# Banded attention with block summaries, then two feed-forward nets: the mask moves into the score products, the block means of v to TensorE

## The chip, the cores and the metric

One core of a Trainium2 chip runs the whole program. The metric is device time in microseconds for one execution. TensorE is called PE below (its sequencer PEq), VectorE DVE, ScalarE ACT, GpSimd POOL, SyncE SP; SP issues nearly all DMAs.

## The reference, cut to what matters

```python
q, k, v: (2, 8, 768, 64); block, window = (32, 16)
k_sum = k.reshape(B, H, nb, block, D).max(axis=3)        # 24 blocks of 32 positions
v_sum = v.reshape(B, H, nb, block, D).mean(axis=3)
scores_l = scale * q @ k^T, kept where |i - j| < 16, else -1e9
scores_s = scale * q @ k_sum^T + log(block)
a = softmax over [scores_l, scores_s]
attn = a @ [v, v_sum]
x = attn as (1536, 512)
h = x @ w_in;  x = (h - tanh(h)) @ w_out                  # d_ff 2048
h = x @ w2_in; out = (h * tanh(softplus(h))) @ w2_out
```

## The kernel before, in words

**Attention.** The 1536 positions are 12 units `u` of 128, six to a batch (`UPB`). A unit needs `kt`, its keys with 16 more at either side and two copies of the 24 block maxima `ksum`; `qt`, its queries; and `vu`, two windows of 96 values, each beside the 24 block means, so 120 rows. `qk(u)` makes the scores of 8 heads in two PSUM tiles, `s` and `tr`, one for each half `e` of the heads: 16 products, 120 columns for each of 4 heads and 2 query halves. `softmax(u, e)` lets DVE add the mask and take the maximum, one head an instruction (line 324), which moves the scores from PSUM into `aa`; ACT then takes the exponentials in `aa` (line 329). `norm` divides by the sums (DVE, then POOL at line 341), `a_trans` transposes on PE and copies to `asb`, `av` multiplies by `vu`, and `x_hi`, `x_lo` split the result into the two parts that the nets read.

**Block means of v.** `load_vt` brings a transposed copy of v in three tiles a batch, `v_sum` adds up 32 columns on DVE or POOL, `v_trans` turns the sums round on PE, ACT writes them into the `vu` buffer of the batch's first unit, and `v_fill` copies them by DMA into the other two of the three `vu` buffers, where they stay for the batch.

**Order.** Nothing reorders: each engine runs its instructions as the code issues them. A loop over steps `j` issues `qk(j/2)` at even `j`, half `e` of a unit's softmax at `j = 2u+1+e`, `norm(u)` at `2u+3`, `a_trans(u, e)` at `2u+5+e`, `av(u)` at `2u+7`, `x_hi(u)` at `2u+8`. `at(j, ...)` hangs loads and sums behind a step, `before_av` puts work ahead of `av`. The first product of the nets (`more_in`) stands at `j = 24`, behind `qk(11)`, `a_trans(9, 0)` and `av(8)`. Each of `s`, `tr`, `aT` and `x` has two PSUM buffers.

**Nets.** From there PE runs 96 steps; a step needs 12 products of 512 columns into the hidden layer and 12 out of it. The weights come as 8-byte numbers and are split on ACT, DVE and POOL, a piece of 256 columns per `conv_tick`; some ticks lie in the attention loop from `j = 19` on.

Of the kernel before, what the change touches and what calls it, by code (L numbers as in the profile page):

```python
# [2 lines left out]

# [18 lines left out]
KW = T + 2 * WIN  # L22
# [4 lines left out]
def kernel(  # L27
# [143 lines left out]
    ASB_DVE = (0, 2, 7, 11, 12, 13, 14, 15, 17, 20, 21)  # L171
    NORM_DVE = (0, 13, 21, 23)
    FILL_DVE = (0, 1, 4, 5, 6, 7, 8, 9, 11)
# [5 lines left out]
    def attention(actx):  # L179
# [7 lines left out]
        qt = [kq.tile([128, HP, 128], F32, name=f"qt{n}") for n in range(3)]  # L187
        vu = [con.tile([KA, 2, H, D], F32, name=f"vu{n}") for n in range(3)]
        masks = [con.tile([128, KA], F32, name=f"mask{m}") for m in range(3)]
# [4 lines left out]
        def constants():  # L194
            nonlocal tops
            make_identity(nc, ident)
            k_edges(0)
            for m in range(3):
                nc.gpsimd.memset(masks[m], 0.0)
                for s in range(2):  # L200
                    rows = masks[m][T * s:T * s + T]
                    nc.gpsimd.memset(rows[:, SUM[s][0]:SUM[s][1]], math.sqrt(D) * math.log(BLK))
                    reg = rows[:, WND[s][0]:WND[s][1]]

                    conds = [([[1, KW]], -1, -1), ([[-1, KW]], 2 * WIN - 1, 1)]
                    if (m, s) == (0, 0):
                        conds.append(([[1, KW]], -WIN, 0))
                    if (m, s) == (2, 1):
                        conds.append(([[-1, KW]], KW - WIN - 1, 0))
                    for pattern, base, mul in conds:  # L210
                        nc.gpsimd.affine_select(
                            out=reg, in_=reg, pattern=pattern, base=base, channel_multiplier=mul,
                            compare_op=ALU.is_ge, fill=-BIG,
                        )
            k_edges(UPB)
            tops = top_tiles(2)

        vtc, ksum, vsum = {}, {}, {}
# [4 lines left out]
        def load_k_own(u):  # L223
            nc.sync.dma_start(
# [14 lines left out]
        def load_q(u):  # L239
            nc.sync.dma_start(out=qt[u % 3], in_=qt_d[u])  # L240

        def load_v(u):
            for s in range(2):
                nc.sync.dma_start(out=vu[u % 3][WND[s][0]:WND[s][1], s], in_=vw_d[u, s])

        def load_vt(b, g):
            vtc[b, g] = two.tile([128, HP, 256], F32, tag="vtc", name="vtc", bufs=3)
# [510 lines left out]
```

## Time and profile before

| what | us |
|---|---|
| median of 3 runs (lowest to highest) | 603.2 (602.33 to 606.38) |
| the profiled execution | 603.07 |
| its span | 601.3 |
| PE busy in the span | 578.8 |

The profiled execution lies 0.13 us under the median and 1.8 us above its own span. Its page gives busy times, the chain that ended last and groups of like instructions; its timeline gives each instruction's start and what it waited for.

### The profile page before, as it was taken

How to read it: one execution, taken by the hardware profiler on the slowest of the kernel's cores; microseconds unless marked ns; L12 is line 12 of the kernel's file. 1: busy time of each engine (PE TensorE's matmuls, PEld its weight loads, DVE VectorE, ACT ScalarE, POOL GpSimd, SP SyncE). 2: the span in 40 equal slices, each digit the busy share in tenths (PEclk: the TensorE clock that was granted, in tenths of full speed). 3: DMA queues.
4: the chain of work that ended last, by engine and by line, in shares of the span. 5: the costliest groups of instructions: out<-in, count | busy, mean ns of one | idle time of the engine just before them, and what ended most of it. 6: DMA issues, size and time to landing. Idle time of an engine off the chain costs nothing.

```text
span 601.3 us, 9203 instructions
## 1 busy us (share of the span) xinstructions
PE 578.8 (96%) x3212; PEld 479.0 (80%) x3212; DVE 417.8 (69%) x968; ACT 328.5 (55%) x791; POOL 53.4 (9%) x109
## 2 busy tenths in 40 slices
PE   6768899999999999999999999999999999999997
PEld 5556788888888888888888888888888888888885
DVE  5797978886251222377776489997688777597785
ACT  4788878885251122367765456664464444454442
POOL 6465660000000000000000000000000000000000
PEclk9798899999999999999999999999999999999999
DMA  9997567765020000226661102100100000100001
GB/s 271 257 306 213 154 184 238 222 218 168 0 88 0 1 0 1 62 88 192 197 186 43 40 8 63 52 2 1 55 16 1 1 1 0 71 1 1 1 1 70
DMA packets 32110, 52.20 MB, mean 87 GB/s; under 512 B 3200, under 2 KB 25728, under 8 KB 32064
## 3 DMA queue, kind: packets, MB, share of 16 engines
q1 hardware_dynamic: 32064, 51.62, 28.5%
q8 instruction: 25, 0.41, 0.3%
q14 instruction: 21, 0.17, 0.1%
HBM read 48.07 MB, written 3.15 MB: 85 GB/s over the span
## 4 chain that ended last, share of the span: by engine, by line
PE 88%; DMA 4%; DVE 3%; ACT 2%; SPq 1%; issue 1%; POOL 0%; ACTq 0%
PE aT L478 7%; PE aT L479 7%; PE tr L479 7%; PE x L479 7%; PE aT L480 7%; PE tr L480 7%; PE x L480 7%; PE x L478 7%; PE tr L478 7%; PE s L479 7%; PE s L478 7%; PE s L480 7%; DMA kt<-in_kw_dram 3%; ACT aa L329 1%; DMA vtc<-in_vt_dram 1%; PE x L363 1%
## 5 line engine op out<-in xcount | busy, mean ns | idle before, releaser
L503 DVE TENSOR_TENSOR glo<-t,ghi 128x512 fp32r<-128x512 f32 x48 | 33.4, 695 | 85.4 <-ACT ghi L498 85.4
L498 ACT ACTIVATE ghi<-t 128x512 fp32r<-128x512 f32 x48 | 30.2, 629 | 96.5 <-PE tr L480 96.5
L478 PE MATMUL aT<-xhi,w 128*128 128x512 f32 x192 | 74.9, 390 | 0.0
L478 PE MATMUL s<-xhi,w 128*128 128x512 f32 x192 | 74.9, 390 | 0.0
L480 PE MATMUL s<-xhi,w 128*128 128x512 f32 x192 | 74.7, 389 | 0.0
L480 PE MATMUL aT<-xhi,w 128*128 128x512 f32 x192 | 74.7, 389 | 0.0
L479 PE MATMUL s<-xlo,w 128*128 128x512 f32 x192 | 74.7, 389 | 0.0
L479 PE MATMUL aT<-xlo,w 128*128 128x512 f32 x192 | 74.7, 389 | 0.0
L114 ACT ACTIVATE top<-raw 128x256 f16<-128x256 bf16 x128 | 61.5, 486 | 12.2 <-ACT w L132 4.8
L121 DVE SCALAR_TENSOR_TENSOR cv<-raw,top 128x256 int32<-128x256 int32 x128 | 55.4, 434 | 11.8 <-ACT top L114 7.6
L132 ACT ACTIVATE w<-cv 128x256 fp32r<-128x256 f32 x120 | 47.6, 402 | 10.7 <-DVE cv L121 9.8
L137 DVE TENSOR_TENSOR w<-cv,w 128x256 fp32r<-128x256 f32 x114 | 48.4, 426 | 0.1
L534 DVE SCALAR_TENSOR_TENSOR t<-n,r 128x512 f32<-128x512 f32 x48 | 33.1, 689 | 17.4 <-ACT r L531 17.3
L503 DVE TENSOR_TENSOR glo<-n,ghi 128x512 fp32r<-128x512 f32 x48 | 33.1, 690 | 15.5 <-ACT ghi L498 15.5
L498 ACT ACTIVATE ghi<-n 128x512 fp32r<-128x512 f32 x48 | 30.3, 632 | 24.4 <-PE tr L479 16.1
L329 ACT ACTIVATE aa<-aa,neg 128x120 f32<-128x120 f32 x96 | 36.6, 384 | 12.4 <-DVE neg L324 12.4
L480 PEld LDWEIGHTS aT<-xhi,w 128*128 128x128 f32 x192 | 36.1, 188 | 7.5
L480 PEld LDWEIGHTS s<-xhi,w 128*128 128x128 f32 x192 | 36.1, 188 | 7.5
L478 PEld LDWEIGHTS aT<-xhi,w 128*128 128x128 f32 x192 | 36.0, 188 | 7.5
L478 PEld LDWEIGHTS s<-xhi,w 128*128 128x128 f32 x192 | 36.0, 188 | 7.5
L479 PEld LDWEIGHTS s<-xlo,w 128*128 128x128 f32 x192 | 36.0, 188 | 7.4
L479 PEld LDWEIGHTS aT<-xlo,w 128*128 128x128 f32 x192 | 36.0, 188 | 7.4
(97 smaller groups left out, 1293.1 us busy)
## 6 DMA issues: line engine op xcount, KB each, us to landing
raw<-in_w_dram SPq DMA_DIRECT2D x128, 255.8 KB, 3.6
vu<-in_vw_dram SPq DMA_DIRECT2D x24, 192.0 KB, 4.9
qt<-in_qt_dram SPq DMA_DIRECT2D x12, 256.0 KB, 4.9
vtc<-in_vt_dram SPq DMA_DIRECT2D x6, 512.0 KB, 6.7
out_dram<-o SPq DMA_DIRECT2D x9, 256.0 KB, 2.0
kt<-in_kw_dram SPq DMA_DIRECT2D x6, 320.0 KB, 8.5
kt<-in_kw_dram SPq DMA_DIRECT2D x6, 256.0 KB
out_dram<-t SPq DMA_DIRECT2D x3, 256.0 KB
```

Source lines behind the costliest of these rows:

```text
L114: nc.scalar.activation(out=tops[n % len(tops)].bitcast(F16).rearrange("p (n t) -> p n t", t=2)[:, :, 1], in_=raws[n].bitcast(BF16).rearran ...
L121: nc.vector.scalar_tensor_tensor(out=tmps[n], in0=raws.pop(n).bitcast(I32).rearrange("p (n t) -> p n t", t=2)[:, :, 0], scalar=13, in1=top ...
L132: nc.scalar.activation(out=hi, in_=t, func=ACTF.Copy)
L137: (nc.gpsimd if on_pool else nc.vector).tensor_tensor(out=W[i][:, 1, o:o + PW], in0=tmps.pop(n).bitcast(F32), in1=W[i][:, 0, o:o + PW].bit ...
L329: nc.scalar.activation(out=aa[u][:, e, hp, :], in_=aa[u][:, e, hp, :], func=ACTF.Exp, scale=-1.0, bias=neg[u][:, e, hp:hp + 1], accum_out= ...
L363: nc.tensor.matmul(out=xps[u][64 * e:64 * e + 64, hp, T * s:T * s + T], lhsT=vu[u % 3][:, s, 2 * hp + e, :], rhs=asb[u, e][:, hp, T * s:T ...
L478: nc.tensor.matmul(out=out, lhsT=w[0], rhs=x[0], start=first, stop=False)
L479: nc.tensor.matmul(out=out, lhsT=w[0], rhs=x[1], start=False, stop=False)
L480: nc.tensor.matmul(out=out, lhsT=w[1], rhs=x[0], start=False, stop=last)
L498: nc.scalar.activation(out=ghi, in_=t, func=ACTF.Copy)
L503: nc.vector.tensor_tensor(out=glo, in0=t, in1=ghi.bitcast(F32), op=ALU.subtract)
L534: nc.vector.scalar_tensor_tensor(out=ts[z], in0=ns[z], scalar=2.0, in1=rs[z], op0=ALU.add, op1=ALU.mult)
```

## The change

- `qk(u)` begins with four bfloat16 products of 480 columns, `sel` times a mask, two into each score tile; the score products accumulate on top. `sel` is an identity of 64 rows over 64 rows of ones, and the mask tile carries the constant of the block scores as three bfloat16 rows whose sum is exact. There are four mask tiles, built on POOL at the start.
- `softmax` becomes `max_(u)`, two reductions over a whole score tile and a small multiplication, both halves at the first odd step, and `exps(u, e)`, which reads the scores in PSUM.
- `vt`, `v_sum` and `v_trans` go. `v_part(b)` multiplies all twelve windows of a batch by small selecting matrices (`means`) into the four 32-row parts of one PSUM tile, ACT copies it out, `v_fold(b)` adds the parts, ACT writes the means into `vu`, and `v_fill` copies them to the other five units of the batch.
- There are 8 `vu` buffers for 3 and 5 `qt` buffers for 3; `k_fill` writes both copies at once, on DVE up to unit 6, then on POOL. The loads stand in another order, half of the first keys are issued by ACT. The tables that gave some copies and normalizations to DVE or ACT go: half 1 of `asb` is DVE's, half 0 ACT's, all normalization POOL's.

```diff
@@ attention
+        NQ, NV = 5, 8
+        means = [con.tile([KA, ZC + 32], F32, name=f"means{s}") for s in range(2)]
+        masks = {z: con.tile([128, KA], BF16, name=f"mask{z[0]}{z[1]}") for z in ((0, 0), (0, 1), (1, 0), (1, 1))}
+        sel = con.tile([128, T], BF16, name="sel")
...
         def load_k_own(u):
-            nc.sync.dma_start(
+            (nc.sync, nc.scalar)[u % 2].dma_start(
...
         def k_fill(u):
-            eng = nc.vector if u in FILL_DVE else nc.gpsimd
-            for o in (0, NB + KU):
-                eng.tensor_copy(kt[u % NK][:, :, o:o + NB], ksum[u // UPB])
+            t = kt[u % NK]
+            o = bass.AP(t.tensor, t.offset, [t.ap[0], [NB + KU, 2], [KU + 2 * NB, HP], [1, NB]])
+            (nc.vector if u <= UPB else nc.gpsimd).tensor_copy(
+                o, ksum[u // UPB].unsqueeze(1).to_broadcast([128, 2, HP, NB])
+            )
+        def v_part(b):
+            p = pst("aT")
+            for k in range(UPB // 2):
+                for t in range(4):
+                    w, s = 2 * k + t // 2, t % 2
+                    nc.tensor.matmul(
+                        out=p[32 * t:32 * t + 32, :],
+                        lhsT=means[s][:, ZC - 4 * w:ZC - 4 * w + 32],
+                        rhs=vu[(b * UPB + w) % NV][:, s].rearrange("p h d -> p (h d)"),
+                        start=k == 0, stop=k == UPB // 2 - 1,
+                    )
+            vpart[b] = two.tile([128, H * D], F32, tag="vp", name="vp", bufs=1)
+            nc.scalar.activation(out=vpart[b], in_=p, func=ACTF.Copy)
+        def v_fold(b):
+            p = pst("aT")
+            nc.tensor.matmul(out=p[0:NB, :], lhsT=fold, rhs=vpart[b])
+            n = b * UPB % NV
             for s in range(2):
                 nc.scalar.activation(
-                    out=vu[0][SUM[s][0]:SUM[s][1], s].rearrange("p h d -> p (h d)"), in_=p[0:NB, :],
+                    out=vu[n][SUM[s][0]:SUM[s][1], s].rearrange("p h d -> p (h d)"), in_=p[0:NB, :],
...
@@ qk
+            for e in range(2):
+                for s in range(2):
+                    m = masks[s, int(w == (0, UPB - 1)[s])]
+                    nc.tensor.matmul(
+                        out=sc[u, e][T * s:T * s + T], lhsT=sel,
+                        rhs=m.unsqueeze(1).to_broadcast([128, HP, KA]), start=True, stop=False,
+                    )
...
+        def max_(u):
+            for e in range(2):
+                nc.vector.tensor_reduce(out=m[:, e], in_=sc[u, e], axis=AX.X, op=ALU.max)
+            nc.vector.tensor_scalar(
+                out=neg[u], in0=m, scalar1=-1.0 / math.sqrt(D), scalar2=None, op0=ALU.mult
+            )
...
-            for hp in range(HP):
-                nc.vector.tensor_tensor_reduce(
-                    out=aa[u][:, e, hp, :], in0=pv[:, hp, :], in1=m, scale=-1.0 / math.sqrt(D),
-                    scalar=3.0e38, op0=ALU.add, op1=ALU.min, accum_out=neg[u][:, e, hp:hp + 1],
-                )
             for hp in range(HP):
                 nc.scalar.activation(
-                    out=aa[u][:, e, hp, :], in_=aa[u][:, e, hp, :], func=ACTF.Exp,
-                    scale=-1.0, bias=neg[u][:, e, hp:hp + 1], accum_out=sums[u][:, e, hp:hp + 1],
+                    out=aa[u][:, e, hp, :], in_=pv[:, hp, :], func=ACTF.Exp,
+                    scale=1.0 / math.sqrt(D), bias=neg[u][:, e, hp:hp + 1],
+                    accum_out=sums[u][:, e, hp:hp + 1],
...
@@ the order of the work
+        before_av[6] = L(v_part, 0)
+        before_av[7] = L(v_fold, 0)
+        at(7, *[L(v_fill, u) for u in range(1, UPB)])
+        at(8, L(load_q, 9), L(k_sum, 6), L(k_sum, 7))
+        at(9, L(load_v, 9), L(k_sum, 8), L(k_sum, 9))
+        at(10, L(load_q, 10), L(k_sum, 10))
+        at(11, L(load_v, 10), L(k_sum, 11), L(k_fill, 6))
...
+        before_av[18] = L(v_part, 1)
+        before_av[19] = L(v_fold, 1)
+        at(19, *[L(v_fill, u) for u in range(UPB + 1, NU)])
```

PE of the kernel before between `a_trans(0, 0)` and `av(0)`: only the four transposed sums stand there, and then the fourth unit's scores (`aT` are transposes, `s` and `tr` scores, `x` the product with `vu_100`, the first `vu` buffer).

```order
L349 MATMUL aT<-ident,aa 120x128 x4
L285 MATMUL tr<-ident,vsum 24x128 x4
L310 MATMUL s<-kt_92,qt_97 64x120
...
L349 MATMUL aT<-ident,aa 120x128 x8
L363 MATMUL x<-asb,vu_100 64x64 x16
L310 MATMUL s<-kt_93,qt_98 64x120
```

PE of the changed kernel from `a_trans(0, 1)` to `qk(4)`; `vu_102` to `vu_107` are the values of the first batch's six units, `vp` the copied-out parts.

```order
L390 MATMUL aT<-ident,aa 120x128 x4
L302 MATMUL aT<-vu_102,means_110 32x512
L302 MATMUL aT<-vu_102,means_111 32x512
...
L302 MATMUL aT<-vu_107,means_111 32x512
L390 MATMUL aT<-ident,aa 120x128 x4
L313 MATMUL aT<-vp,fold 24x512
L404 MATMUL x<-asb,vu_102 64x64 x16
L339 LDWEIGHTS sel
L339 MATMUL s<-mask_113,sel 64x480
```

Twelve products of 512 columns and the fold now stand behind the fourth unit's scores and ahead of `av(0)`, `av(0)` ahead of the fifth unit's mask and scores.

DVE of the changed kernel around the maxima of the fifth unit (`max` and `neg`), from the copy `asb(1, 1)` on.

```order
L394 COPY asb<-aT 120x512
L283 TENSOR_REDUCE ksum<-kt_95 128x4x4
L283 TENSOR_REDUCE ksum<-kt_96 128x4x4
L358 TENSOR_REDUCE max<-s 128x4
L358 TENSOR_REDUCE max<-tr 128x4
L359 TENSOR_SCALAR neg<-max 128x8
```

DVE of the kernel before at the fifth unit: the maxima of its two halves stand apart, each behind one block maximum.

```order
L255 TENSOR_REDUCE ksum<-kt_90 128x4x4
L324 ISA aa,neg<-s,mask_104 128x120
L324 ISA neg 128x1
...
L375 TENSOR_TENSOR xlo_70<-x,xhi_67 128x4x128
L255 TENSOR_REDUCE ksum<-kt_91 128x4x4
L324 ISA aa,neg<-tr,mask_104 128x120
```

So a copy that waits for PE and two block maxima now stand ahead of all eight heads' maxima.

SP of the changed kernel, from the last of the loads that nothing holds up to the first fills.

```order
L253 DMA kt_95<-in_kw_dram 128x4x160
L253 DMA kt_96<-in_kw_dram 128x4x160
L253 DMA kt_89<-in_kw_dram 128x4x160
L253 DMA kt_90<-in_kw_dram 128x4x160
L253 DMA kt_91<-in_kw_dram 128x4x160
L253 DMA kt_92<-in_kw_dram 128x4x160
L276 DMA vu_108<-in_vw_dram 96x512 x2
L276 DMA vu_109<-in_vw_dram 96x512 x2
L272 DMA qt_97<-in_qt_dram 128x512
...
L324 DMA vu_103<-vu_102 24x512 x2
```

The fill that `av(1)` reads (`vu_103`) is issued behind the keys of all twelve units, eight units' values and nine units' queries (9.04 MB); before, it stood behind nine, three and six of them and three tiles of transposed v (6.88 MB).

## Rows read from the trace of the kernel before

**Rows 1.** The profile page: the span and each engine's busy time.

```profile
span 601.3 us, 9203 instructions
...
PE 578.8 (96%) x3212; PEld 479.0 (80%) x3212; DVE 417.8 (69%) x968; ACT 328.5 (55%) x791; POOL 53.4 (9%) x109
```

**Rows 2.** Stretches: busy time by engine, granted PE clock, DMA share, GB/s.

```profile
20.40:25.00 4.60, 3.48 (x41) 2.93 (x40) 1.70 (x11) 2.01 (x8) 1.75 (x2) 0.71 1.08 300
...
47.80:53.00 5.20, 4.48 (x77) 3.63 (x76) 3.90 (x22) 3.41 (x16) 1.70 (x6) 0.82 0.94 214
```

**Rows 3.** PE's timeline: start, duration, operation, count, wait before it.

```profile
41.47 0.31 PE L310 MATMUL s<-kt,qt 64*64 64x120 f32 x1
...
42.45 1.09 PE L349 MATMUL aT<-ident,aa 128*120 128x128 f32 x8
...
47.81 0.46 PE L310 MATMUL s<-kt,qt 64*64 64x120 f32 x1
...
49.62 1.09 PE L349 MATMUL aT<-ident,aa 128*120 128x128 f32 x8
...
62.11 1.15 PE L363 MATMUL x<-asb,vu 120*64 120x64 f32 x30 [1.65 <-DVE asb L353]
...
68.29 0.50 PE L478 MATMUL s<-xhi,w 128*128 128x512 f32 x1
...
71.14 0.60 PE L349 MATMUL aT<-ident,aa 128*120 128x128 f32 x4
...
76.76 0.62 PE L349 MATMUL aT<-ident,aa 128*120 128x128 f32 x4 [0.16 <-POOL aa L341]
```

**Rows 4.** ACT's timeline: the first exponential of units 0, 3, 4, 6 and 9.

```profile
11.47 0.40 ACT L329 ACTIVATE aa<-aa,neg 128x120 f32<-128x120 f32 x1 [2.44 <-DVE neg L324]
...
26.45 0.39 ACT L329 ACTIVATE aa<-aa,neg 128x120 f32<-128x120 f32 x1
...
30.43 0.39 ACT L329 ACTIVATE aa<-aa,neg 128x120 f32<-128x120 f32 x1
...
40.69 0.38 ACT L329 ACTIVATE aa<-aa,neg 128x120 f32<-128x120 f32 x1
...
57.31 0.40 ACT L329 ACTIVATE aa<-aa,neg 128x120 f32<-128x120 f32 x1 [0.59 <-DVE neg L324]
```

**Rows 5.** Groups of instructions, first 150 us: busy and mean | idle before, releaser.

```profile
L329 ACT ACTIVATE aa<-aa,neg 128x120 f32<-128x120 f32 x96 | 36.6, 384 | 12.4 <-DVE neg L324 12.4
...
L341 POOL TENSOR_TENSOR aa<-aa,rd 128x480 f32<-128x480 f32 x20 | 20.8, 1055 | 22.8 <-DVE rd L339 10.1 <-ACT aa L329 6.5 <-PE x L363 5.9
...
L375 DVE TENSOR_TENSOR xlo<-x,xhi 128x512 fp32r<-128x512 f32 x12 | 7.9, 660 | 0.0
...
L355 ACT ACTIVATE asb<-aT 120x512 f32<-120x512 f32 x13 | 7.5, 581 | 0.3 <-PE aT L349 0.3
L353 DVE COPY asb<-aT 120x512 f32<-120x512 f32 x11 | 7.4, 674 | 2.9 <-PE aT L349 2.9
...
L272 DVE TENSOR_REDUCE vsum<-vtc 128x16 f32<-128x512 f32 x7 | 4.7, 679 | 0.0
...
L211 POOL TENSOR_SCALAR_AFFINE_SELECT mask<-mask 64x96 f32<-64x96 f32 x14 | 3.7, 261 | 0.8
```

**Rows 6.** DVE's timeline: two block sums together, a small multiplication, a fill.

```profile
17.67 1.28 DVE L272 TENSOR_REDUCE vsum<-vtc 128x16 f32<-128x512 f32 x2
...
19.67 0.17 DVE L336 TENSOR_SCALAR rd<-sums 128x8 f32<-128x8 f32 x1
...
35.30 0.33 DVE L263 COPY kt<-ksum 128x96 f32<-128x96 f32 x2
```

**Rows 7.** The chain that ended last, two pieces; and the tile `vu`: shortest/median/longest ns.

```profile
0.74 0.69 SPq L224
...
14.94 8.57 DMA kt<-in_kw_dram
...
L294 SPq DMA_DIRECT2D vu<-vu x8: 714/750/892, 21.3 to 56.9; - x8
```

More of the change, by code (lines that the diff above doesn't have):

```diff
@@ L186, in attention @@
         kt = [kq.tile([128, HP, KU + 2 * NB], F32, name=f"kt{n}") for n in range(NK)]
[L187 to L189 removed]
+        NQ, NV = 5, 8
+        qt = [kq.tile([128, HP, 128], F32, name=f"qt{n}") for n in range(NQ)]
+        vu = [con.tile([KA, 2, H, D], F32, name=f"vu{n}") for n in range(NV)]
+        ZC = 4 * (UPB - 1)
+        means = [con.tile([KA, ZC + 32], F32, name=f"means{s}") for s in range(2)]
+        fold = con.tile([128, NB], F32, name="fold")
+        masks = {z: con.tile([128, KA], BF16, name=f"mask{z[0]}{z[1]}") for z in ((0, 0), (0, 1), (1, 0), (1, 1))}
+        sel = con.tile([128, T], BF16, name="sel")
         ident = con.tile([128, 128], F32, name="ident")
@@ new lines, in constants @@
+            k_edges(UPB)
+            for n in range(NV):
+                for s in range(2):
+                    (nc.vector, nc.gpsimd)[s].memset(vu[n][SUM[s][0]:SUM[s][1], s], 0.0)
+            for s in range(2):
+                nc.gpsimd.memset(means[s], 0.0)
+                cols = means[s][:, ZC + 2 * s:ZC + 2 * s + 2]
+                nc.gpsimd.memset(cols, 1.0 / BLK)
+                own = WND[s][0] + WIN
+                for pattern, base, mul in (([[-BLK, 2]], -own, 1), ([[BLK, 2]], own + BLK - 1, -1)):
+                    nc.gpsimd.affine_select(
+                        out=cols, in_=cols, pattern=pattern, base=base, channel_multiplier=mul,
+                        compare_op=ALU.is_ge, fill=0.0,
+                    )
@@ L216, in constants @@
+            nc.gpsimd.tensor_tensor(out=fold, in0=ident[:, 0:NB], in1=ident[:, 32:32 + NB], op=ALU.add)
+            for t in (2, 3):
+                nc.gpsimd.tensor_tensor(out=fold, in0=fold, in1=ident[:, 32 * t:32 * t + NB], op=ALU.add)
             tops = top_tiles(2)
-        vtc, ksum, vsum = {}, {}, {}
+        ksum, vpart = {}, {}
         def load_k(u):
@@ L388, in attention @@
         load_q(0)
-        load_vt(0, 0)
-        load_q(1)
-        load_v(0)
-        load_vt(0, 1)
-        load_q(2)
-        load_vt(0, 2)
+        for u in range(4):
+            load_v(u)
+            load_q(u + 1)
+        for u in (4, 5):
+            load_v(u)
+        for u in (6, 7):
+            load_k(u)
         constants()
```

135 lines of the change are left out of this document (52 added, 83 removed).

## Prediction

> **What bounds the kernel now.** I read the page first. PE is busy for 578.8 of 601.3 us [rows 1], and the nets' products are most of that. PE's timeline tells where the rest lies: the first product of the nets starts at 68.29 us [rows 3], and from there on PE hardly waits before the output (0.16 us ahead of the transpose at 76.76 [rows 3]). The change leaves those 96 steps as they are. So the execution lasts 603.07 - 68.29 = 534.8 us from the nets' first product on, and the question is when that product starts. Everything below is about the attention stage.
>
> In that stage no engine is full. The stretches show PE busy for 3.48 of 4.60 us and 4.48 of 5.20, with a granted clock of 0.71 and 0.82 [rows 2]; ACT needs 0.38 us for each of 96 exponentials and waits 12.4 us for DVE's maxima [rows 5]. The first exponential comes at 11.47, the fourth unit's at 26.45, the fifth's at 30.43, the seventh's at 40.69, the tenth's at 57.31 [rows 4]: 5.5 us a unit in the middle ((57.31 - 40.69) / 3). Loads fill the DMA engines early: 300 GB/s at a full share [rows 2], and one tile of keys took 8.57 us to land on the chain [rows 7].
>
> **The change part by part.** A duration runs some 0.1 us into the next instruction of its engine (two reductions of 0.68 [rows 5] take 1.28 [rows 6]), so I count 0.1 less than the means of [rows 5] for all but the exponentials.
>
> Maxima. Before, eight instructions a unit on DVE, and ACT could begin 0.3 us after the scores. Now two reductions of 480 columns; the nearest row has two of 512 in 1.28 us, and the multiplication 0.17 [rows 6]. With hand-overs 1.45 us, and ACT begins only when all are done. So the first exponential moves from 11.47 to about 12.7.
>
> Exponentials. They read PSUM, not SBUF; ACT's copies out of PSUM, 512 columns in 0.58 [rows 5], give no reason for another price, so 0.38 each, four in 1.52. What moves is when `s` and `tr` come free: after ACT, not after DVE.
>
> Mask products. PE ran twelve products of 512 columns in 71.14 - 68.29 = 2.85 us, 0.24 each [rows 3]; four of 480 cost 0.86 one behind the other and 0.43 if the two halves of the output rows run together, as those of `av` do. I take 0.65. The scores took 42.45 - 41.47 = 0.98 and, at the low level of the clock, 49.62 - 47.81 = 1.81 [rows 3].
>
> Means of v. No row has four 32-row outputs at once. 32 score instructions (16 products in two passes, four side by side) of 120 columns took 0.98 us; 24 instructions of 512 columns cost 24 x 512/120 x 0.98/32 = 3.1 us at that rate. From `av`, whose products overlap in pairs (30 instructions of 64 columns in 1.15 us [rows 3]), it is 24 x 8 x 1.15/30 = 7.4, and with no overlap some 12.4 (four times 3.1). I take 3.3, nearest to the scores, since these too lie in four parts of the output rows or of the array. The Trainium skill (TensorE: Matmul & The Clock Gate, Part 3, measured speedup) has three products of 32 output rows side by side at 2.38 times the speed of one, not 3. By that four would cost 12.4 / 3.2 = 3.9, and my forecast would be 2 us later; no run shows it yet. On ACT it adds a copy (0.50) and two copies into `vu` (0.98, as before).
>
> What goes: 3.1 MB of `vt`, 10 us of DMA at 300 GB/s [rows 2], and seven block sums on DVE, 0.64 each by [rows 6], with POOL's five. None of it stands on the chain that I follow from 12.7 on, except through the loads, which step (4) counts. The four masks, the memsets and `fold` make some 52 small instructions on POOL, 13.5 us at the 0.26 of a select [rows 5]. The first two masks wanted are done near 7 us, ahead of the first scores, and the rest ahead of the first normalization at 16 us, so they cost nothing; at one and a half times that price normalization would begin 4 us late, and the first transposes with it.
>
> Now the chain, step by step, at a granted clock of 0.91 (PE's prices times 1.1). (1) Units 0 to 2: 24 exponentials from 12.7 with a copy (0.48): ACT is free at 22.5. (2) The scores of unit 3 wait for unit 1's last exponential (18.9), the means stand behind them: scores to 20.4, transposes to 20.9, means to 24.3, copy to 24.8. ACT has waited 1.7. Unit 3 starts at 24.8, 1.6 us ahead of before (26.45 [rows 4]). (3) ACT: 1.52, a copy 0.48, both copies into `vu` 0.98: 27.8. PE: `av(0)` 1.2, masks and scores of unit 4 1.9, transposes 0.5: 31.5. DVE: the copy 0.6, two block maxima 1.28, the maxima 1.45: unit 4 starts at 34.9. Before it was 30.43: 4.5 behind. ACT has run dry at 31.2, with `x_hi(0)` and unit 3's second half done. (4) `av(1)` needs the fill, which lands behind 9.04 MB: at 300 GB/s, from an estimated 2.5 us on (the first issue stands at 0.74 [rows 7]), that is 32.6, and 1 more to land: 33.7, while PE is there at 32.1. `av(1)`, masks, scores, transposes to 37.3; DVE's copy, a block maximum, maxima: unit 5 at 40.1. The ten fills cost SP 0.75 us each to issue [rows 7]; queued behind them are only loads of values and queries for unit 8 on, 10 us early. (5) Unit 6's scores need `k_fill(6)`, which stands on DVE behind unit 5's maxima (40.0), the reciprocals 0.37, `x_lo` 0.58, a block maximum 0.62 and itself 0.33 [rows 5, 6]: 41.9. Scores 1.2, transposes 0.5, copy 0.6, maxima 1.5: unit 6 at 45.95, before 40.69 [rows 4]: 5.3 behind. (6) Then PE's round sets the pace: masks 0.7, scores 1.1, two transposes 1.2, `av` 1.2, hand-over 0.1: 4.3 us, above ACT's 3.04 + 0.48 + 0.48 = 4.0. That gives 1.2 us a unit back against 5.5: unit 9 at 58.9, and with the second batch's means (a wait of 1.2 and a copy) 60.6, before 57.31: 3.3 behind. (7) ACT: 1.52 + 0.48 + 0.98 to 63.6; `av(6)` to 64.9; two rounds of PE, each masks to `av`: the nets start at 73.6, where before had 68.29: 5.3 us late.
>
> (8) Behind that, `a_trans(11, .)` waits for POOL, which now does both halves (1.0 us each [rows 5]) among the weight pieces; before, DVE did one and PE still waited 0.16 us [rows 3]. I add 1.0.
>
> Sum: 534.8 + 73.6 + 1.0 = 609.4 us. The profiled execution stands 0.13 under the median, so that is also the median's forecast. Its own bounds: full clock, masks at 0.43 and means at 3.1 give a start at 70.9 and 606; masks at 0.86, means at 3.7 give 76.7 and 612.5.
>
> **The rivals.** *The waits are hidden.* If PE's round is 3.6 us (full clock, masks 0.43) and `k_fill(6)`, fill and means come early enough, ACT alone sets the pace: unit 3 at 22.5, seven units at 4.0 and twice 1.5 us of copies for the means end unit 9's exponentials at 53.5; with 3.7 us of PE behind them the nets start at 57.2, and the time is 593. It decides from the point where DVE reaches the fifth unit's maxima before 31.2, when ACT runs dry. For it speaks that ACT's 4.0 is far under 5.5; against it that step (3) is a string of in-order pieces with no slack in it. Half of that gain gives 600.
>
> *The low clock.* The clock was 0.71 from 20.4 to 25, after PE had waited [rows 2], and scores at that level took 0.83 us more [rows 3]. The change puts waits of 2 us on PE ahead of `av(0)`, `av(1)` and `qk(6)`. If each sends it down for a round, a round costs 2 to 2.5 us more: three of them, 6 us, 615. The Trainium skill (TensorE: Matmul & The Clock Gate, Part 1) says that an idle PE falls back to half its rate; the trace agrees as far as 0.71 there and 1.81 for the scores go. Late loads would act the same way: a fill 3 us later is 3 us.
>
> *The parts of the means don't overlap.* Then each batch's means cost 7.4 to 12.4 us on PE, in front of `av` and of all scores behind: 4 to 9 us more, twice: 618 to 627.
>
> **How the numbers follow.** Forecast (606 to 613): 0.52. Waits partly or all hidden (593 to 606): 0.22. Clock or loads (613 to 618): 0.16. No overlap (beyond 618): 0.10. About one per cent, 6 us, is what a measurement of this kernel can tell from no change; the forecast lies just at it. Below 597: 0.09. Up to 609.2 are 0.13 of the hidden waits and half of the forecast, 0.40 together. Above: 0.51. The range from 598 to 618 leaves out 0.1 on either side.
>
> **What would show it.** In the changed profile the nets' first product should start at 71 to 77 us and the rest last 535 to 536. ACT should wait 3 to 4 us ahead of the fifth unit's exponentials, with the releaser a DVE maximum; PE should wait for a fill or for ACT's `vu` copy ahead of `av(0)` and `av(1)`, and for DVE's fill ahead of the seventh unit's scores. The means should span 3 to 4 us with four instructions starting together; if they start one by one, the third rival holds. If unit 4 starts near 31 instead of 35, the first one does. I am wrong altogether if the stretch after the nets' start has gaps, from weights that come late.

## The result, and the profile after

The changed kernel takes 612.3 us (median of 4 runs, 612.02 to 612.63) where the kernel before, run beside it, took 603.0: a ratio of 1.014 (95% interval 1.0105 to 1.0181), 9 us or 1.4% slower. The forecast was 609.4 with a range from 598 to 618.

The profiled execution took 612.02 us. Its page begins (span, then busy time by engine; [rows 1] are those of before):

```profile
span 610.3 us, 9240 instructions
...
PE 588.6 (96%) x3304; PEld 479.4 (79%) x3304; DVE 411.4 (67%) x799; ACT 325.6 (53%) x792; POOL 53.3 (9%) x111
```

PE's timeline of the changed kernel (start, duration, operation, count, wait before it), which answers to [rows 3]:

```profile
10.43 0.31 PE L348 MATMUL s<-kt,qt 64*64 64x120 f32 x1 [1.28 <-DVE kt L291]
...
23.48 2.78 PE L302 MATMUL aT<-vu,means 120*32 120x512 f32 x24 [0.33 <-ACT asb L396]
...
27.06 1.04 PE L313 MATMUL aT<-vp,fold 128*24 128x512 f32 x2 [0.21 <-ACT vp L309]
29.34 0.34 PE L404 MATMUL x<-asb,vu 120*64 120x64 f32 x4 [1.24 <-ACT vu L316]
...
30.82 0.38 PE L339 MATMUL s<-mask,sel 128*64 128x480 bf16 x2
...
31.32 0.31 PE L348 MATMUL s<-kt,qt 64*64 64x120 f32 x1
...
35.63 1.24 PE L404 MATMUL x<-asb,vu 120*64 120x64 f32 x32 [2.23 <-DMA vu<-vu]
...
44.09 0.31 PE L348 MATMUL s<-kt,qt 64*64 64x120 f32 x1 [2.91 <-DVE kt L291]
...
45.07 1.96 PE L390 MATMUL aT<-ident,aa 128*120 128x128 f32 x8
...
76.58 0.50 PE L514 MATMUL s<-xhi,w 128*128 128x512 f32 x1
```

The nets' first product comes at 76.58 us where it came at 68.29 [rows 3]: 8.3 us of the 9. What follows takes 612.02 - 76.58 = 535.4 us, against 534.8. Nearly all of the loss lies in the attention stage. The three waits that the prediction named are there: `av(0)` for ACT's copies into `vu` (1.24), `av(1)` for the fill (2.23), the seventh unit's scores for DVE's fill of the keys (2.91). The masks take 0.5 us from their first to the scores; the means' 24 instructions take 2.78.

ACT's timeline, the first exponentials of units 0, 3, 4, 5, 6, 9 and 10, as in [rows 4]:

```profile
14.70 0.36 ACT L369 ACTIVATE aa<-s,neg 128x120 f32<-128x120 f32 x1 [5.73 <-DVE neg L359]
...
26.91 0.35 ACT L369 ACTIVATE aa<-s,neg 128x120 f32<-128x120 f32 x1
...
36.32 0.36 ACT L369 ACTIVATE aa<-s,neg 128x120 f32<-128x120 f32 x1 [3.33 <-DVE rd L377]
...
41.61 0.36 ACT L369 ACTIVATE aa<-s,neg 128x120 f32<-128x120 f32 x1 [1.47 <-DVE rd L377]
...
48.36 0.36 ACT L369 ACTIVATE aa<-s,neg 128x120 f32<-128x120 f32 x1 [2.92 <-DVE rd L377]
...
62.27 0.35 ACT L369 ACTIVATE aa<-s,neg 128x120 f32<-128x120 f32 x1
...
72.08 0.36 ACT L369 ACTIVATE aa<-s,neg 128x120 f32<-128x120 f32 x1 [3.15 <-DVE rd L377]
```

The releaser is put down as DVE's `rd`, which runs just behind the maxima (`neg`, L359); it is the maxima that ACT waits for. Where nothing stands between two units they follow at 3.9 us (units 7 and 8 start at 52.94 and 56.84), faster than the 5.5 of before. Unit 4 comes 9.4 us behind unit 3, unit 10 comes 9.8 behind unit 9, and both times the means lie between; unit 6 comes 6.75 behind unit 5.

DVE's timeline, at the start, ahead of the fifth unit's maxima, and at the fill of the seventh unit's keys:

```profile
9.85 3.42 DVE L291 COPY kt<-ksum 128x192 f32<-128x192 f32 x6
13.19 0.64 DVE L358 TENSOR_REDUCE max<-s 128x4 f32<-128x480 f32 x1
...
33.00 0.69 DVE L394 COPY asb<-aT 120x512 f32<-120x512 f32 x1 [7.45 <-PE aT L390]
33.60 1.27 DVE L283 TENSOR_REDUCE ksum<-kt 128x16 f32<-128x512 f32 x2
34.79 0.65 DVE L358 TENSOR_REDUCE max<-s 128x4 f32<-128x480 f32 x1
...
43.00 1.03 DVE L291 COPY kt<-ksum 128x192 f32<-128x192 f32 x1
```

The fifth unit's scores are done at 32.3 (the transposes start behind them then), but DVE waits for the copy of transposes and does two block maxima first, and begins with that unit's own at 34.79: the string that step (3) drew. Two things here are not in the prediction: six fills of keys take 3.42 us at the start, and one takes 1.03 at 43.00, for 0.33 by [rows 6]. POOL's timeline at those two places:

```profile
8.80 4.35 POOL L233 MEMSET vu<- 24x512 f32 x8
...
41.99 1.93 POOL L382 TENSOR_TENSOR aa<-aa,rd 128x480 f32<-128x480 f32 x2 [3.36 <-DVE rd L380]
```

DVE's fill at 43.00 ends at 44.03, just behind POOL's second multiplication (43.92); the six at the start run beside POOL's memsets.

### The profile page after: what moved, and what is told of

Its sections match the earlier page's. It is cut to its first block, busy times and chain, and to the rows that moved or that the text cites. A ratio compares the mean times of both kernels' runs of the same rounds, so it can differ in the third digit from the quotient of the medians.

```text
span 610.3 us, 9240 instructions
## 1 busy us (share of the span) xinstructions
PE 588.6 (96%) x3304; PEld 479.4 (79%) x3304; DVE 411.4 (67%) x799; ACT 325.6 (53%) x792; POOL 53.3 (9%) x111
## 4 chain that ended last, share of the span: by engine, by line
PE 89%; DVE 4%; DMA 3%; ACT 3%; issue 0%; POOL 0%; SPq 0%; ACTq 0%
PE aT L514 7%; PE aT L515 7%; PE x L515 7%; PE tr L515 7%; PE aT L516 7%; PE tr L514 7%; PE x L516 7%; PE tr L516 7%; PE x L514 7%; PE s L516 7%; PE s L515 7%; PE s L514 7%; ACT aa L369 2%; PE x L404 1%; DVE max L358 1%; DMA vu<-in_vw_dram 1%
## 5 line engine op out<-in xcount | busy, mean ns | idle before, releaser
L123 DVE SCALAR_TENSOR_TENSOR cv<-raw,top 128x256 int32<-128x256 int32 x128 | 56.4, 442 | 15.8 <-ACT top L116 12.2
L555 ACT ACTIVATE t<-aT 128x512 f32<-128x512 f32 x24 | 14.4, 599 | 44.6 <-PE aT L516 29.1
```

What stands on the lines that cost most here:

```text
L123: nc.vector.scalar_tensor_tensor(out=tmps[n], in0=raws.pop(n).bitcast(I32).rearrange("p (n t) -> p n t", t=2)[:, :, 0], scalar=13, in1=top ...
L555: nc.scalar.activation(out=t, in_=hs[z], func=ACTF.Exp)
```

## The experiments

Executions of one kernel spread by up to 0.8% here (605.72 to 610.38 for one of them), more than some edits are worth. So each run is also read by the start of the nets' first product in its profiled execution. What follows that product took 535.1 to 536.4 us in all twelve runs and 535.4 in the changed kernel, so a microsecond there is a microsecond of time within some 1.3 us. All ratios are against the kernel before, run beside.

A caution goes with these starts. In the changed kernel unit 10 comes 9.8 us behind unit 9, and PE's granted clock is low there, 0.50 from 66 to 68 us. In runs 1, 2, 4, 5 and 9, which have the same work at that place, the clock is full and the gap is 8.2; run 9, for one (columns as in [rows 2]):

```profile
60.00:70.00 10.00, 9.09 (x182) 7.06 (x182) 7.45 (x14) 7.19 (x31) 4.47 (x7) 1.00 0.29 68
```

So 1.6 us of what those runs gain on 76.58 lie in this stretch, and no run shows that their edits are what keeps the clock up. Ahead of it, at unit 9 (62.27 in the changed kernel), run 1 is 2.4 us earlier, run 2 is 0.4 later, run 4 is 1.3 later and run 9 is 5.5 earlier.

**1. Block maxima early.**

```diff
-        at(8, L(load_q, 9), L(k_sum, 6), L(k_sum, 7))
-        at(9, L(load_v, 9), L(k_sum, 8), L(k_sum, 9))
-        at(10, L(load_q, 10), L(k_sum, 10))
-        at(11, L(load_v, 10), L(k_sum, 11), L(k_fill, 6))
+        at(7, *[L(k_sum, u) for u in range(6, 12)], L(k_fill, 6))
+        at(8, L(load_q, 9))
+        at(9, L(load_v, 9))
+        at(10, L(load_q, 10))
+        at(11, L(load_v, 10))
```

> The second batch's six block maxima and the fill of unit 6 move from DVE's steps 8 to 11 to step 7, into a stretch in which DVE of the changed kernel stood idle (25.5 to 33.0 us). Theory of the order (DVE's in-order stream keeps the maxima of unit 4 and the scores of unit 6 waiting): unit 4's first exponential 1.2 us earlier (35.1 for 36.32), unit 5's 0.6 earlier (41.0), the 2.91 us wait ahead of unit 6's scores gone, nets' first product at about 73.6 for 76.58, time about 609. Rival, the fill of v sets the pace from unit 5 on and PE's round the rest: unit 6's scores start no more than 1 us earlier than 44.09 and the time stays at 611.5 to 612.5. Rival on the price of that fill: 1.03 us on DVE in the changed kernel because POOL was multiplying at the same time; here POOL is idle, so 0.4 or less; if the copy's shape is the reason, 1.0 again.

Measured: 608.3 us, ratio 1.0074 (1.0051 to 1.0098); nets' first product at 72.62, 4.0 us earlier (1.6 of them at the stretch named above). DVE and PE of this run:

```profile
32.20 0.26 DVE L291 COPY kt<-ksum 128x192 f32<-128x192 f32 x1
33.19 0.69 DVE L394 COPY asb<-aT 120x512 f32<-120x512 f32 x1 [0.73 <-PE aT L390]
33.80 0.65 DVE L358 TENSOR_REDUCE max<-s 128x4 f32<-128x480 f32 x1
...
37.15 1.22 PE L404 MATMUL x<-asb,vu 120*64 120x64 f32 x32 [3.55 <-DMA vu<-vu]
```

The wait ahead of the seventh unit's scores is gone (unit 6 comes 3.9 us behind unit 5, 46.42 for 42.52), unit 4 starts at 35.34. The order of DVE's work is shown as a cause. The fill takes 0.26 us where POOL is idle. Unit 5 did not come earlier (42.52 for 41.61): the fill of v, which landed 1.5 us later here, holds it.

**2. The fills of v ahead of later loads.**

```diff
-        at(6, L(load_v, 6), L(load_v, 7), L(load_q, 5), L(load_q, 6), L(load_q, 7), L(load_q, 8))
+        at(6, L(load_q, 5), L(load_q, 6))
...
+        at(7, L(load_v, 6), L(load_v, 7), L(load_q, 7), L(load_q, 8))
         at(7, L(load_v, 8))
```

> Two units' values and two units' queries (1.3 MB) are loaded behind the five fills of v and no longer ahead of them. If the fill lands late because it is queued behind loads: the wait of 2.23 us ahead of the second unit's product with v is gone or under 0.5, that product starts near 33.5 for 35.63, unit 5 near 39.6 for 41.61, nets' first product near 74.6, time about 610. If the fill's own way through the queue takes the 5.4 us: the product starts at 35 or later and the time stays within 0.7 of 612.3.

Measured: 610.2 us, ratio 1.0096 (1.0065 to 1.0126); nets' first product at 75.39, 1.2 us earlier, all of it behind unit 9. The second unit's product starts at 34.04 without a wait, so the fill was late because of the loads ahead of it, as step (4) had it. But unit 5 starts at 41.62 as before the edit: DVE, with its three block maxima between the maxima of units 4 and 5, comes to unit 5's maxima at 40.09, in the changed kernel at 40.08. Fill and block maxima were two waits side by side.

**3. Without the means of v.**

```diff
-        before_av[6] = L(v_part, 0)
-        before_av[7] = L(v_fold, 0)
-        at(7, *[L(v_fill, u) for u in range(1, UPB)])
...
-        before_av[18] = L(v_part, 1)
-        before_av[19] = L(v_fold, 1)
-        at(19, *[L(v_fill, u) for u in range(UPB + 1, NU)])
```

> Leaves out the block means of v altogether: the products with the selecting matrices, the fold, ACT's three copies a batch and the fills; the rows of vu that hold the means stay zero, so the block part of the attention's product is missing. This is the price of the new way to the means. Theory: the steps 3 to 4 and 9 to 10 of the units (9.4 and 9.8 us in the changed kernel against 3.9 to 4.3 where nothing stands between) lose 3 to 5 us each: nets' first product at 66 to 68, time 601 to 603. Rival, the waits of unit 4 and unit 10 are of DVE's and PE's order and the means only fill them: nets' first product at 73 or later, 609 or more.

Measured: 603.9 us, ratio 1.000 (0.998 to 1.002); nets' first product at 67.80. The means with their fills cost 8.8 us of the first product's start, and without them the changed kernel is level with the one before. In time it is 1.0143 for 1.000 by the two ratios, 8.6 us. The clock's stretch behind unit 9, low in the changed kernel and full here, can be part of the 8.8. On the other side, in this run PE waits 3.18 us ahead of the sixth unit's scores for queries that the changed kernel has in time.

**4. ACT zeroes `vu` in POOL's place.**

```diff
-                for s in range(2):
-                    (nc.vector, nc.gpsimd)[s].memset(vu[n][SUM[s][0]:SUM[s][1], s], 0.0)
+                nc.vector.memset(vu[n][SUM[0][0]:SUM[0][1], 0], 0.0)
...
         for u in range(UPB):
             k_fill(u)
+        for n in range(NV):
+            nc.scalar.copy(vu[n][SUM[1][0]:SUM[1][1], 1].rearrange("p h d -> p (h d)"), zero[SUM[1][0]:SUM[1][1]])
```

> POOL's eight memsets of vu go (ACT copies zeros there instead, ahead of its first exponential, where it stood idle); all else is as in the changed kernel. If the copies of DVE that fill the keys (0.57 us each) were held up by POOL's memsets beside them: they take 0.3 us or less each, six of them 1.8 or less for 3.42, and the first exponential comes 1.6 to 2.3 us earlier, near 12.7. If the shape of the copy is the reason: 0.57 again, first exponential at 14.7. For the time: the fill of v still lands at about 35, so I expect no more than 1 us of it to be left at the nets' first product (75.6 to 76.6; 611.3 to 612.3); the rival, that the stage is a chain from its first exponential on, gives 74.6 and 610.3.

Measured: 613.6 us, ratio 1.0154 (1.0120 to 1.0187), above the 611.3 to 612.3 that I expected; nets' first product at 76.30. DVE's timeline, ACT's first exponential, and PE at the second unit's product:

```profile
9.97 1.18 DVE L292 COPY kt<-ksum 128x192 f32<-128x192 f32 x6
11.38 0.66 DVE L359 TENSOR_REDUCE max<-s 128x4 f32<-128x480 f32 x1 [0.23 <-PE tr L349]
...
13.46 0.36 ACT L370 ACTIVATE aa<-s,neg 128x120 f32<-128x120 f32 x1
...
35.42 1.98 PE L405 MATMUL x<-asb,vu 120*64 120x64 f32 x32 [3.64 <-DMA vu<-vu]
```

The same six fills take 1.18 us for 3.42. So POOL's memsets of `vu` were what held them, and the shape of the copy was not. The first maxima come 1.8 us earlier, the first exponential 1.2 (ACT's own zeroing ends at 13.45). Of this 0.3 us is left at the nets: the second unit's product waits 3.64 us for the fill instead of 2.23 and starts at 35.42 instead of 35.63, since SP issues the fill at 30.02, behind its loads, whenever the copies into `vu` are done. The 0.3 us is no clean price: behind the longer wait the clock is low from 34 to 42 us, where it was full, and unit 5 comes 2.2 us later (43.81); the gap behind unit 9 (8.2 us for 9.8) gives part of that back.

**5. Both edits, 1 and 2.** The two diffs above in one kernel.

> The two edits of the first round together: block maxima early and the fills of v ahead of the later loads. Alone, the first moved the nets' first product from 76.58 to 72.62 and left a wait of 3.55 us for the fill ahead of the second unit's product with v; the second took that wait away, but unit 5's maxima came no earlier (40.09 in both), since DVE's block maxima took as long, and moved the first product to 75.39 only. If fill and block maxima were two waits side by side, of which only the later counted, then with both gone the 3.55 us come back whole: unit 5 at 39.0 or earlier for 42.52, nets' first product near 69.2 (69 to 70), 604 to 605.5. If the gains only add: 71.4, 607.

Measured: 606.5 us, ratio 1.0066 (1.0042 to 1.0089); nets' first product at 72.77. Units 5 and 6 come at 39.18 and 43.29, 3.3 and 3.1 us ahead of run 1, so the two waits do stand side by side. Then the gain is lost, and the start is later than either case that I had named. PE:

```profile
45.59 0.43 PE L348 MATMUL s<-kt,qt 64*64 64x120 f32 x1 [2.14 <-DMA qt<-in_qt_dram]
```

These are unit 7's queries, which edit 2 had put behind ten fills; unit 7 comes at 50.69, 7.4 us behind unit 6.

**6. Without the mask products.** The loop over `masks` in `qk` is left out, and the score products start their PSUM regions themselves.

> Leaves out the four mask products of each unit (the window and the constant of the block scores are not added, so the attention sums over keys that should be masked). This is the price of the mask on PE, 0.65 us a unit in the prediction, with four products seen to start in pairs 0.2 us apart. If it counts in every round: 12 x 0.5 = 6 us, nets' first product at 70.5, 606. If it is hidden wherever ACT, DVE or a fill sets the pace, which is the case in half of the units: 2 us, 74.5, 610. If in all: 76.6, 612.

Measured: 611.4 us (609.33 to 614.46), ratio 1.0157 (1.0113 to 1.0201); nets' first product at 73.88, 2.7 us earlier, nearest to the middle case. Its times do not show that gain (its median is 2 us above its profiled execution), so the 2.7 us rests on the trace alone. It is 0.2 us a unit, less than half of the 0.5 that the masks take on PE. And 2.0 of the 2.7 come between units 9 and 10 (7.8 us for 9.8), where the changed kernel's clock was low, so the price of the masks is bounded by this run and not measured.

**7. The mask part alone, in the kernel before.** `max_`, `exps`, the four masks and the mask products replace `softmax` and its three masks; everything else is as before the change.

> The kernel before with the mask part of the change alone: mask products on PE, maxima of four heads at once, exponentials from PSUM; loads, transposed v, block sums and all tables stay as they were. The run without the means came out level with the kernel before, so I expect this one within 2 us of it too: first exponential 1 to 1.5 us later (12.5 to 13), units at ACT's shorter price (0.335 for 0.384 us an exponential), nets' first product at 67 to 70, 602 to 605. Rival, maxima of all eight heads at once cost by themselves, 1 us in each of the units where DVE is behind: nets' first product at 72 or later, 607 or more.

Measured: 606.0 us, ratio 1.0043 (1.0023 to 1.0064); nets' first product at 71.86, 1.9 us outside of what I expected and 0.14 short of the rival's 72. The first exponential comes at 12.75, 1.3 us later than before, as priced, and by unit 3 that is made up (26.55 for 26.45 [rows 4]). Most of the loss comes at the second batch: unit 9 starts at 62.60 for 57.31, after ACT has waited 3.77 us ahead of unit 8 and 3.31 ahead of unit 9. There a copy of transposes stands ahead of the maxima on DVE:

```profile
60.45 0.69 DVE L374 COPY asb<-aT 120x512 f32<-120x512 f32 x1 [4.34 <-PE aT L370]
61.06 0.65 DVE L338 TENSOR_REDUCE max<-s 128x4 f32<-128x480 f32 x1
```

The kernel before has that copy at the same place. Its row, and the masks of the tenth unit in this run:

```profile
56.31 0.69 DVE L353 COPY asb<-aT 120x512 f32<-120x512 f32 x1 [1.63 <-PE aT L349]
...
57.35 0.39 PE L319 MATMUL tr<-mask,sel 128*64 128x480 bf16 x2 [2.31 <-ACT vu L297]
```

So the copy is not new, but ACT's first exponential comes 2.15 us behind its start for 1.00 before (57.31), and at unit 8 2.74 for 1.57: some 1.2 us each, now that all eight heads' maxima come first. Another part stands on PE: the masks wait 2.31 us for ACT, where the scores of the kernel before wait 1.18, and the granted clock is 0.57 from 57.9 to 61.9, where it was full.

So the mask part moves the nets' first product by 3.6 us with the tables of the kernel before. How much of it is the order of DVE's work and how much the clock was not tried. With the 8.8 us of run 3 it makes more than the whole 8.3, so what a part costs depends on what stands beside it; the other parts (buffers, loads, tables) were not run alone.

**8. The means a step or two ahead.**

```diff
@@ v_part, v_fold
-            p = pst("aT")
+            p = pst("x")
@@ the order of the work
-        before_av[6] = L(v_part, 0)
-        before_av[7] = L(v_fold, 0)
+        before_av[5] = L(v_part, 0)
+        before_av[6] = L(v_fold, 0)
...
-        before_av[18] = L(v_part, 1)
-        before_av[19] = L(v_fold, 1)
-        at(19, *[L(v_fill, u) for u in range(UPB + 1, NU)])
+        before_av[16] = L(v_part, 1)
+        before_av[17] = L(v_fold, 1)
+        at(17, *[L(v_fill, u) for u in range(UPB + 1, NU)])
```

> Only the place of the means of v: products and fold one step earlier for the first batch (steps 5 and 6), two steps earlier for the second (16 and 17, with its fills), both in the PSUM buffers of the product with v, so that they wait for no copy of transposes. Theory: what the means cost is the chain of products, copy, fold, two copies and the product with v, which ACT's second half of units 3 and 9 stands behind (31.53 and 67.46 in the changed kernel); with it a step or two ahead, the second batch's 3 to 4 us (unit 10 at 9.8 us behind unit 9, for 3.9 to 4.3 elsewhere) are gone and of the first batch's little, since the fill still lands at 35: nets' first product at 72 to 74, 607.5 to 609.5. Rival, the means cost by the work that they add to PE and ACT, 2.7 and 2.2 us a batch, wherever it stands: 76 to 77, 612.

Measured: 612.4 us, ratio 1.0158 (1.0129 to 1.0188); nets' first product at 77.95, neither of the two. In the second batch the theory held: unit 9 comes 6.4 us behind unit 8 and unit 10 4.9 behind unit 9, together 11.35 us for the 15.24 of the changed kernel (some 1.6 of the difference lie where its clock was low). The first batch lost what this gained and more. The means now stand ahead of the fourth unit's scores and take 3.97 us there, the first part at the low clock; the keys that are loaded into that unit's buffer wait for those scores, SP issues the fills behind them (at 31.97 for 30.22), and the second unit's product waits 5.49 us, to 37.75.

**9. Both edits, with unit 7's queries in front again.** The first line of edit 2 becomes `at(6, L(load_q, 5), L(load_q, 6), L(load_q, 7))`.

> As the run with both edits, but the queries of unit 7 are loaded ahead of the fills again. That run lost 2.14 us of PE's time waiting for these queries, and its unit 7 came 7.4 us behind unit 6 for 3.9 to 4.3 elsewhere. If this wait is where the gain of the two edits went, unit 7 comes 4 us behind unit 6 and the nets' first product stands at 69 to 70 for 72.77, 603.5 to 605.5. If the second batch's means or PE's clock take it back, 71.5 or later.

Measured: 605.6 us, ratio 1.0054 (1.0035 to 1.0073); nets' first product at 69.55, as expected, and the profiled execution took 604.97. Unit 7 comes 3.9 us behind unit 6. So two moves in the order of loads and block maxima, with no work removed, take 7.0 us off the start of the nets' first product, 5.5 of them by unit 9. The two ratios (1.0143 and 1.0054) give some 5.4 us of time, and their intervals allow for either. What is left are the means: units 4 and 10 still come 8.2 us behind units 3 and 9 (35.31 for 27.07, 65.05 for 56.81).

**10. The edits together, with the second batch's means ahead.** Run 9 with the last two block maxima and the fill at step 9, the zeroing on ACT for six buffers and on DVE for two, and steps 16 and 17 for the second batch's means.

> Every edit that gained alone: block maxima early (the last two behind unit 4's maxima), fills of v ahead of the later loads with unit 7's queries ahead of them, ACT and DVE zeroing vu in POOL's place, and the second batch's means two steps earlier. Counted from 69.3 for the run before it in this round: the second batch 3.4 (unit 10 at 6.4 us behind unit 9 for 9.8, as in the run with the means ahead), the earlier first exponential up to 1.0 now that no fill holds the second unit up: nets' first product at 65 to 66, 600 to 601.5, level with or a little under the kernel before. If earlier starts are again lost to a fill or a load: 66.5 to 68, 602 to 603.5.

Measured: 607.2 us, ratio 1.0071 (1.0056 to 1.0086); nets' first product at 71.79: a miss. Up to unit 7 it runs 0.4 to 1.0 us ahead of run 9 (46.80 for 47.23). Then PE stands at the means, which take 6.6 us (48.82 to 55.41) for 2.78, for values that are not there yet:

```profile
51.09 1.88 PE L305 MATMUL aT<-vu,means 120*32 120x512 f32 x4 [0.34 <-DMA vu<-in_vw_dram]
53.75 1.66 PE L305 MATMUL aT<-vu,means 120*32 120x512 f32 x4 [0.79 <-DMA vu<-in_vw_dram]
```

In run 8 the same steps came 9.9 us later (58.68 for 48.82), and the values were there.

**11. The first product with v put off, first try.** Run 10, with `av(0)` at step 8 behind the fifth unit's scores.

> The tuned kernel, and for the first batch the product of unit 0 with v stands behind unit 4's scores (step 8 for 7), with ACT's copy of it behind unit 3's exponentials, and unit 4's maxima directly behind its scores. If the first batch's means cost 4 us because unit 4's scores stand behind the product that waits for ACT's copies into vu: unit 4 comes 5.5 to 6.5 us behind unit 3 for 8.2, the nets' first product 1.5 to 2.5 us ahead of the tuned kernel's, 598.5 to 600. If PE's and ACT's work is what fills that stretch: within 0.5 us of the tuned kernel.

Measured: 619.2 us, ratio 1.0269 (1.0254 to 1.0285). The load of unit 8's values, which goes into unit 0's buffer, stayed at step 7. In this kernel it therefore comes ahead of the product that was put off: the product waits for it (15.35 us, to 44.70) and multiplies unit 8's values in place of unit 0's. The run tells nothing of the theory.

**12. The product put off for both batches, with that load behind it.** Run 10 with the second batch's means back at steps 18 and 19, and:

```diff
-            if xu >= 0 and not xr:
+            if xu >= 0 and not xr and xu % UPB:
                 x_hi(xu)
             if j < NJ and j % 2 == 0:
                 qk(j // 2)
+            if j in (8, 20):
+                max_(j // 2)
...
-            if LA <= j < NJ + LA and (j - LA) % 2:
+            if LA <= j < NJ + LA and (j - LA) % 2 and (j - LA) // 2 % UPB:
                 av((j - LA) // 2)
+            if j in (8, 20):
+                av(j // 2 - 4)
+                x_hi(j // 2 - 4)
```

(`max_` no longer runs at steps 9 and 21, and unit 8's values are loaded at step 8.)

> The tuned kernel with the second batch's means back at steps 18 and 19, and for both batches the first unit's product with v behind the scores of the fifth unit (steps 8 and 20 for 7 and 19; the load of unit 8's values, which overwrites unit 0's, moves behind it), ACT's copy of it behind the exponentials of the unit before, and the maxima of units 4 and 10 directly behind their scores. In the run with both edits and unit 7's queries ahead, which has its nets' first product at 69.55, units 4 and 10 come 8.2 us behind units 3 and 9, since their scores stand behind a product that waits for the means' last two copies on ACT. If that order is the price of the means, the two gaps become 5.5 to 6.5, the nets' first product comes at 64 to 66, and the time is 600 to 602, level with the kernel before or a little under. If it is the work itself (products, fold and three copies), the gaps stay at 7.7 to 8.2, and the first product at 68.5 to 69.5, 604 to 605.

Measured: 601.7 us against 604.3 for the kernel before beside it, ratio 0.9956 (0.9936 to 0.9976): 0.4% faster than the kernel before and, by the two ratios against it (0.9956 / 1.0143), 1.8% faster than the changed kernel. ACT's first exponentials of units 3, 4, 9 and 10, and the nets' first product; behind them DVE's first maximum of the fifth unit:

```profile
26.75 0.35 ACT L372 ACTIVATE aa<-s,neg 128x120 f32<-128x120 f32 x1
31.66 0.36 ACT L372 ACTIVATE aa<-s,neg 128x120 f32<-128x120 f32 x1
...
56.44 0.36 ACT L372 ACTIVATE aa<-s,neg 128x120 f32<-128x120 f32 x1
61.98 0.37 ACT L372 ACTIVATE aa<-s,neg 128x120 f32<-128x120 f32 x1
67.38 0.50 PE L527 MATMUL s<-xhi,w 128*128 128x512 f32 x1
...
29.51 0.66 DVE L361 TENSOR_REDUCE max<-s 128x4 f32<-128x480 f32 x1 [1.07 <-PE tr L351]
```

The two gaps are 4.9 and 5.5 us for 8.2, the first under what I expected and the second at its edge, with the same products, fold and copies. So the order in which the means stand made these two gaps. It is not shown that it makes most of what the means cost. The first product comes 2.2 us ahead of run 9, of which up to 1.0 is the earlier first exponential, and 1.4 us behind the range that I gave, since other waits came up: unit 5 waits 2.1 us for its maxima and comes 5.9 us behind unit 4 for 3.9, PE waits 0.73 for unit 8's queries, and the second batch's means take 3.60 us. A kernel with these edits and without the means, which would give the price of their work, was not run.

## Why the prediction came out

The forecast of 609.4 was 2.9 us short, within its range, and with the sign right. Its mechanism, in-order engines that wait where the means, the block maxima and the fills stand, is what the runs show; the sizes of three terms were off. It came closer than its terms, and that is luck: in the table below stretches forecast too short make 4.4 us, stretches forecast too long 1.8. Forecast and measured length of each stretch of the sum (us):

| stretch | forecast | measured |
|---|---|---|
| to the first exponential | 12.7 | 14.7 |
| to unit 3 | 12.1 | 12.2 |
| unit 3 to 4, steps (2) and (3) | 10.1 | 9.4 |
| unit 4 to 5, step (4) | 5.2 | 5.3 |
| unit 5 to 6, step (5) | 5.85 | 6.75 |
| unit 6 to 9, step (6) | 14.65 | 13.9 |
| unit 9 to the nets, step (7) | 13.0 | 14.3 |
| the rest, with step (8) | 535.8 | 535.4 |

- *Constants on POOL "cost nothing".* This term failed. The masks were done in time, but the memsets of `vu` among these constants ran beside DVE's fills of keys and stretched them from 1.18 to 3.42 us (run 4), which put the first exponential 2.0 us behind the forecast. Taking the memsets away gave 0.3 us at the nets and nothing in time (run 4), since the fill of v was later still: forecast to land at 33.7, it released PE at 35.63, 5.4 us behind its issue. For the 1 us from the last load to its landing the prediction had no row. With the fill early DVE's block maxima keep unit 5 where it was (run 2).
- *`k_fill(6)` at 0.33.* It took 1.03 beside POOL's multiplication and 0.26 without (run 1): 0.7 of the 0.9 us by which step (5) was short. The trace of before had this price too: the fill at 35.30 that [rows 6] shows had POOL idle beside it, and another, beside the same multiplication, took 1.11:

```profile
41.64 1.94 POOL L341 TENSOR_TENSOR aa<-aa,rd 128x480 f32<-128x480 f32 x2 [0.55 <-PE x L363]
...
42.53 1.11 DVE L263 COPY kt<-ksum 128x96 f32<-128x96 f32 x2
```

- *A clock of 0.91 throughout.* It was either full (1.00) or at its low level (0.50). Busy time by engine, granted clock, DMA share and GB/s of the changed kernel in a stretch at full clock, in the one behind the 2.91 us wait, and in the one behind the waits of 1.24 and 0.27 ahead of `av(6)`:

```profile
31.00:34.00 3.00, 2.40 (x44) 1.67 (x40) 1.00 (x2) 1.96 (x9) 0.00 (x0) 1.00 0.95 296
45.00:48.60 3.60, 3.60 (x48) 3.19 (x42) 2.32 (x7) 0.68 (x4) 0.00 (x0) 0.53 0.85 219
64.70:69.20 4.50, 4.22 (x68) 3.21 (x68) 0.43 (x1) 3.37 (x12) 0.40 (x1) 0.62 0.20 47
```

  The eight transposes took 1.96 us in the second for 1.09; in the third, masks and scores took 2.5 us (66.71 to the transposes at 69.25) for 1.5 (30.82 to 32.31). That is where step (7)'s 1.3 us went, as far as these rows show; the full clock elsewhere makes up for what step (6) had too much, at a round of 3.9 to 4.6 us for 4.3. The rival of the low clock was thus in part there, with two stretches of some 1.5 us and not three of 2 to 2.5. A third lies ahead of unit 3, at unit 2's scores (1.87 us at 18.02 for 1.05). A wait alone does not tell where: the same 1.24 and 0.27 ahead of `av(0)` left the clock full.
- *Means on PE, 3.3 us.* 2.78. The third rival, no overlap, fell. The estimate of 3.9 from the Trainium skill's speedup (TensorE: Matmul & The Clock Gate, Part 3, measured speedup) was too high too: two instructions of the fold take 1.04 us, the second 0.44 behind the first, and 24 at that distance would take 10.6, so four side by side ran at 3.8 times the speed of one, where the page has 2.38 for three.
- *Masks, 0.65 a unit.* 0.5 on PE, of which at most 0.2 reach the end (run 6).
- *Maxima.* 1.4 us from the first reduction to the end of `neg`, for 1.45. That ACT can begin only behind all of them cost what was forecast at the start (1.3 us in run 7), and more where a copy stands ahead of them on DVE.
- *Exponentials.* They follow each other at 0.335 us from PSUM (14.70, 15.05, 15.38) and not at 0.38; over eight a unit that is 0.4 us in ACT's favour, which the forecast left out.
- *Step (8).* The wait of `a_trans(11, .)` for POOL is on the chain that ended last, and the rest grew by 0.66 for the 1.0 that I gave it. The chain's pieces there (start, us, what):

```profile
84.82 1.00 POOL aa L382
85.82 0.04 issue
85.86 0.65 PE aT L390 x4
```

- *Sums.* Step (5)'s terms add up to 45.7 and not 45.95, the lower of the two bounds to 606.7 and not 606, and means at 3.9 for 3.3 make the forecast 1.3 us later and not 2.
- *The waits are hidden.* This rival, 593 to 606, fell for the kernel as changed. It named the right condition: with DVE at the fifth unit's maxima at 29.51 instead of 34.79, ahead of 31.2, run 12 lies in its range.

## What to carry to other kernels

A new step on an in-order engine is priced by what it stands in front of: here 12 products, a fold and three copies a batch cost 8.8 us where they were put, 7.0 of the 8.3 us that the nets began late came back with block maxima and loads moved alone (1.6 of the 7.0 in the stretch where the clock differs), and all of them with the zeroing, a product and a set of maxima moved as well, no work removed. A price read from one row holds for what stood beside that row: the same pair of copies cost 0.33 us with POOL idle and 1.1 beside POOL's multiplication. Two waits side by side show a gain only when both are gone, so an edit that takes away its wait and moves the end by little is not refuted; look which wait is now the last. A place in the order that works in one schedule is bought with its delays: after each gain the loads have to be looked at again, since they are what comes next.

## What the runs showed of the hardware that was not expected

- A copy from SBUF to SBUF on DVE can be held up by POOL. The fill of keys took 0.57 us beside memsets of `vu` on POOL and 0.20 without them, and 1.03 beside a multiplication of POOL, ending 0.11 us behind it. Not all work of POOL does it: the six fills of run 4, at 0.20 each from 9.97 to 11.15, ran beside POOL's short selects and small additions such as this one:

```profile
10.56 0.68 POOL L248 TENSOR_TENSOR fold<-fold,ident 128x24 f32<-128x24 f32 x2
```

  The reductions did not suffer: two block maxima took 1.20 us beside POOL's selects at 5.17 and 1.27 at 33.60, with POOL idle, and four took 2.46 at 7.35, the last beside a memset of `vu`. The Trainium skill (SBUF — State Buffer, Who interferes with whom) says that the two engines share a pair of ports, which a copy in a fast mode of DVE or an instruction of POOL holds for its whole length, and that reductions on trn2 don't contend; the rows beside the memsets and the multiplication and those of the reductions agree, and the six fills of run 4 show no such wait.
- Four outputs of 32 rows side by side ran at nearly four times the speed of one in float32 (2.78 us for 24 instructions of 512 columns).
- ACT's exponentials of 120 columns are 0.05 us shorter out of PSUM than in place in SBUF (one each 0.335 us for 0.38), with the sum taken along in both.
